# One emission table for all five engines in the leading part of an attention and two-FFN kernel

## The chip, the cores and the metric

The kernel runs on one core of one Trainium2 chip. The metric is the device time of one execution in microseconds (us). The engines are called as the profile calls them: PE (matrix products), DVE (VectorE), ACT (ScalarE), POOL (GpSimd), SP (the queue that issues DMAs). Each engine executes its own instructions in a fixed order; between engines, semaphores make one wait for another.

## The reference

A chunked linear attention is followed by two feed-forward layers over the same 3072 tokens (4 batches of 768, model width 256):

```python
L = np.exp(cum[:, :, :, None] - cum[:, :, None, :]) * causal
CB = np.einsum('bhin,bhjn->bhij', Cc, Bc)
y_intra = np.einsum('bhij,bhjd->bhid', CB * L, xc)
y_inter = np.einsum('bhin,bhnd->bhid', Cc, state) * decay_to_i[:, :, :, None]
y[:, :, sl] = y_intra + y_inter
state = decay_full * state + np.sum(Bx, axis=2)
...
x1 = (1 / (1 + np.exp(-(x @ w_gate))) * (x @ w_val)) @ w_out
h = x1 @ w_in
out = (h / (1 + np.exp(-h))) @ w2_out
```

The weights come as 64-bit floats. The kernel turns each slice into 32-bit floats with integer operations and splits it, like every activation, into a high and a low part, so that three products (high by high, high by low, low by high) stand for one.

## The kernel before, in words

**Attention** runs over 24 chunks q of 128 tokens. For a chunk, DMAs bring B and C (`bc`), `x` and the decays, broadcast to a 128x1024 tile `L`. A scan on DVE (line 338) makes the decay matrix in place; PE makes C·B (`cb`, two halves), DVE multiplies each half into `L` (line 383); PE then makes `y` from `L` and `x`, and, within a batch, from the running state `S` and the weighted C (`cwT`). POOL makes the weighted B and C (`bw`, `cw`); DVE updates the state (lines 421/423, 435). `y` is one PSUM tile with one buffer: ACT copies its high part to `xT0` (line 450) and DVE writes the low part to `xT1` (line 451), and only then may the next chunk's `y` begin. From chunk 4 on, B and C reach the products through bf16 tiles (`st`, filled by ACT and DVE, line 323) that DMA transposes turn (`tr`). `L` has four buffers, so the DMA of chunk q+4 can't start before chunk q's `y` is made.

**First layer.** Tokens form blocks b of 2, 2, 4, 4, 4, 4, 4 chunks. For each block and each f of 12 slices of the hidden width, PE makes a gate (`g`, six products) and a value (`v`, six), ACT the sigmoid, DVE their product `sg` (line 530); ACT rounds it to `gh`, DVE makes the rest `gl` (line 539), and PE adds the six products of `m1_out` to `acc`. For blocks 0 and 1 and f below 7 the output weights and `sg` stay whole, and `m1_out` has two f32 products; a later step, `w1_split` (DVE line 222), splits these weights.

**Weight conversion** (`conv`): for each f three DMAs fill `raw` (four buffers); ACT two steps, DVE two (lines 177, 178), POOL one or two additions, ACT the high part, DVE the low part (line 188).

**Second layer**, the same way with 16 slices, over six blocks of 512 tokens.

**What sets the order.** All steps are Python calls. A list of steps (attention by `slot_steps`, conversions placed by the table `WPOS`) is drained between the `g`, `v` and `o` calls of a tick (b, f), so many each time as `RUNS` says for blocks 0 and 1, and an even rate after that. The order of SP is the order of the calls (`manual_schedule` for SP alone); on PE, DVE, ACT and POOL the framework's scheduler orders the instructions when the program is built. On the chip the order of every engine is fixed.

Of the kernel before, what the change touches and what calls it, by code (L numbers as in the profile page):

```python
# [8 lines left out]
F32 = mybir.dt.float32  # L9
# [14 lines left out]
NX = 4  # L24
# [8 lines left out]
WPOS = [  # L33
    0, 0, 0, 22, 25, 31, 31, 31, 31, 31, 31, 31, 32, 32, 32, 32, 32, 32, 32, 32, 32, 34, 34, 34, 34, 34, 35,
    35, 35, 35, 35,
]

RUNS = [
# [3 lines left out]
]  # L42
# [3 lines left out]
def tile_linattn_moe_moe(  # L46
# [89 lines left out]
    def zeros(n, out=None, start=True):  # L136
        if out is None:
            out = acc[0][:, 1] if 0 in acc else ps[:, 1]
        n_ = out.shape[-1]
        last = pe_last[0]  # L140
        with tc.issue_after(last) if last is not None else nullcontext():
            for _ in range(n):
                nc.tensor.matmul(
                    out, zz[:, :P], zz[:, :n_], start=start, stop=start, skip_group_check=True
                )

    pe_last = [None]
# [17 lines left out]
    def conv(raw, hi, lo, n, whole=None):  # L165


# [17 lines left out]
        nc.gpsimd.tensor_tensor(ti, ti, r, ALU.add)  # L185
        with tc.issue_after(stg["behind"]) if "behind" in stg else nullcontext():
            nc.scalar.copy(hi, f)
        nc.vector.tensor_sub(lo, f, hi.bitcast(F32))

    def load_w(w, f, ins, outs, native=None):  # L190

        nonlocal cnt
        cnt += 1
        n = DM * (len(ins) + 1)
        raw = stg["p"].tile([P, 2 * n], I32, tag="raw", name=f"raw{cnt}", bufs=stg["raw"])
        fs = slice(f * P, (f + 1) * P)
        for z, m in enumerate(ins):
# [28 lines left out]


# [26 lines left out]
    def at_load(q):  # L254
        at_load_bc(q)
        at_load_x(q)

    def at_load_bc(q):
# [6 lines left out]
        nc.sync.dma_start(out=bc[:, 0], in_=B[b, :, sl, :].rearrange("h s n -> s h n"))  # L265
        nc.sync.dma_start(out=bc[:, 1], in_=C[b, :, sl, :].rearrange("h s n -> s h n"))
# [8 lines left out]
    def at_wide1(q):  # L275
# [627 lines left out]
```

## Time and profile before

| quantity | value |
|---|---|
| median of 3 runs | 663.72 us (662.73 to 664.83) |
| the profiled execution, its own time | 663.99 us |
| its span, first to last instruction | 662.2 us |
| mean granted PE clock | 0.992 of full speed |
| PE busy | 635.5 us (96% of the span) |
| DVE busy | 432.8 us (65%) |
| ACT busy | 329.0 us (50%) |
| POOL busy | 108.7 us (16%) |

The span and the execution's own time differ by 1.8 us that lie around the instructions. "Busy" counts the time from an instruction's start to its end; a share of the whole span is a mean over stages that have different limits, so the sections below ask for stretches.

### The profile page before, as it was taken

To read this page: it belongs to the slowest core of one execution; us is meant where nothing else is said; L and a number is where in the kernel's file an instruction comes from. 1 tells how busy PE (TensorE), PEld (TensorE's weight loads), DVE (VectorE), ACT (ScalarE), POOL (GpSimd) and SP (SyncE) were. 2 spreads that over 40 slices of the span, in tenths; PEclk is the share of its full clock that TensorE was granted. 3 is DMA by queue.
4 is the path that set the end of the run, shared out by engine and by line. 5 is a ranking of instruction groups with operands and counts; after the bars stand their busy time and mean duration, and the time that the engine had idled before them with its cause. 6 is when DMAs were issued, how large, how long until landed. Compare 5 with 4: busy or idle time off the path is not lost.

```text
span 662.2 us, 9861 instructions
## 1 busy us (share of the span) xinstructions
PE 635.5 (96%) x3680; PEld 522.0 (79%) x3682; DVE 432.8 (65%) x660; ACT 329.0 (50%) x649; POOL 108.7 (16%) x129
## 2 busy tenths in 40 slices
PE   5788898999999999999999999999999999999998
PEld 2477796777778787787888878888888888888886
DVE  8988987676768578656348885564564655544644
ACT  5675554544544554434336664544554544444543
POOL 4555432211221222311002410000000000000000
PEclk9998999999999999999999999999999999999999
DMA  8958577774656365342002410000000000000000
GB/s 207 267 146 212 89 158 154 153 128 109 120 121 145 77 145 119 81 125 75 0 1 66 157 33 1 1 32 1 1 32 1 1 32 1 33 0 1 33 0 33
DMA packets 140145, 51.18 MB, mean 77 GB/s; under 512 B 119009, under 2 KB 133537, under 8 KB 140097
## 3 DMA queue, kind: packets, MB, share of 16 engines
q1 hardware_dynamic: 139952, 50.41, 32.1%
q8 instruction: 29, 0.48, 0.3%
q14 instruction: 20, 0.16, 0.1%
q10 hardware_dynamic: 144, 0.13, 0.1%
HBM read 36.80 MB, written 3.24 MB: 60 GB/s over the span
## 4 chain that ended last, share of the span: by engine, by line
PE 79%; DVE 4%; DMA 4%; issue 3%; POOL 2%; ACT 1%; SPq 0%; DVEq 0%; POOLq 0%; ACTq 0%
PE h L509 20%; PE o L807 13%; PE v L509 11%; PE acc L558 11%; PE g L509 11%; PE o L828 7%; DMA raw<-in_moe_w_out_dram 3%; PE y L398 2%; DMA L<-ac_d 1%; POOL cvt L185 1%; PE cb L381 1%; PE y L392 1%; DVE sg L530 1%; DVE cvt L178 1%; DVE L L338 1%
## 5 line engine op out<-in xcount | busy, mean ns | idle before, releaser
L509 PE MATMUL v<-xT,w 128*128 128x512 f32 (+1 forms) x504 | 119.4, 369 | 3.9 <-ACT sg L522 2.4
L509 PE MATMUL g<-xT,w 128*128 128x512 f32 (+1 forms) x504 | 120.8, 370 | 0.0
L782 DVE TENSOR_TENSOR sh<-h,sh 128x512 f32<-128x512 f32 x96 | 66.2, 691 | 63.2 <-ACT sh L781 61.7
L509 PE MATMUL h<-x2T,w2b 128*128 128x512 f32 x432 | 107.0, 389 | 0.0
L791 DVE TENSOR_TENSOR gl<-sh,gh 128x512 fp32r<-128x512 f32 x96 | 65.8, 690 | 58.4 <-ACT gh L786 56.9
L509 PEld LDWEIGHTS v<-xT,w 128*128 128x128 f32 x504 | 87.4, 192 | 19.3 <-ACT sg L522 3.0
L509 PEld LDWEIGHTS g<-xT,w 128*128 128x128 f32 x504 | 87.7, 191 | 16.3 <-issue 1.5
L558 PE MATMUL acc<-gh,w 128*128 128x512 f32 (+1 forms) x280 | 94.5, 380 | 0.2 <-ACT x1T L569 0.2
L781 ACT ACTIVATE sh<-h 128x512 f32<-128x512 f32 x96 | 57.5, 599 | 73.3 <-PE h L509 70.2
L509 PEld LDWEIGHTS h<-x2T,w2b 128*128 128x128 f32 x432 | 80.7, 188 | 16.5
L786 ACT CAST gh<-sh 128x512 fp32r<-128x512 f32 x96 | 59.0, 620 | 62.2 <-PE o L807 31.0
L503 ACT CAST gh<-sg 128x512 fp32r<-128x512 f32 (+1 forms) x70 | 41.2, 588 | 93.6 <-DVE sg L530 93.6
L807 PE MATMUL o<-w2b,gh 128*128 128x512 f32 x280 | 74.2, 390 | 0.0
L530 DVE TENSOR_TENSOR sg<-v,sg 128x512 f32<-128x512 f32 (+1 forms) x84 | 50.8, 607 | 30.4 <-PE v L509 29.5
L539 DVE TENSOR_TENSOR gl<-sg,gh 128x512 fp32r<-128x512 f32 (+1 forms) x70 | 50.6, 723 | 23.3 <-ACT gh L503 23.0
L338 DVE TENSOR_TENSOR_SCAN L<-L,eye 128x1024 f32<-128x1024 f32 x24 | 55.2, 2302 | 16.0 <-DMA L<-ac_d 15.9
L185 POOL TENSOR_TENSOR cvt<-cvt,raw 128x512 int32<-128x512 int32 (+1 forms) x28 | 46.5, 1664 | 98.7 <-DVE cvt L178 81.5
L522 ACT ACTIVATE sg<-g 128x512 f32<-128x512 f32 (+1 forms) x84 | 44.8, 534 | 31.5 <-PE g L509 28.6
L558 PEld LDWEIGHTS acc<-gh,w 128*128 128x128 f32 x280 | 52.3, 190 | 9.9 <-ACT x1T L569 0.3
L807 PEld LDWEIGHTS o<-w2b,gh 128*128 128x128 f32 x280 | 51.8, 188 | 10.3
L558 PE MATMUL acc<-gl,w 128*128 128x512 f32 (+1 forms) x140 | 53.3, 380 | 1.0 <-DVE gl L539 1.0
L828 PEld LDWEIGHTS o<-w2b,gl 128*128 128x128 f32 x288 | 36.9, 191 | 1.3
(95 smaller groups left out, 724.9 us busy)
## 6 DMA issues: line engine op xcount, KB each, us to landing
L<-ac_d SPq DMA_DIRECT2D x23, 512.0 KB, 4.7
raw<-in_moe_w_out_dram SPq DMA_DIRECT2D x28, 256.0 KB, 3.9
raw<-in_moe_w_in_dram SPq DMA_DIRECT2D x16, 256.0 KB, 2.8
x<-in_x_dram SPq DMA_DIRECT2D x24, 128.0 KB, 3.1
raw<-in_moe_w_gate_dram SPq DMA_DIRECT2D x12, 256.0 KB, 4.4
raw<-in_moe_w_val_dram SPq DMA_DIRECT2D x12, 256.0 KB, 4.7
out_dram<-o2t SPq DMA_DIRECT2D x20, 128.0 KB, 1.7
bc<-in_B_dram SPq DMA_DIRECT2D x24, 64.0 KB, 2.7
```

The lines of the kernel that those rows point to most:

```text
L185: nc.gpsimd.tensor_tensor(ti, ti, r, ALU.add)
L338: nc.vector.tensor_tensor_scan(t["Lf"], t["Lf"], eye, 0.0, op0=ALU.mult, op1=ALU.add)
L509: nc.tensor.matmul(psum[:, :n], w[:, i, o + k * P : o + (k + 1) * P], xt[j][:, k, :n], start=(z == 0), stop=(z == len(k_terms) - 1),)
L530: nc.vector.tensor_mul(sg[:, :n], ps[:, :n], sg[:, :n])
L539: nc.vector.tensor_sub(lo[:, :n], sg[:, :n], hi[:, :n].bitcast(F32))
L558: mm = nc.tensor.matmul(o, v[:, ms], g[:, :n], start=(f == 0 and z == 0 and not (small and m)), stop=(f == NF1 - 1 and z == len(terms) - 1 ...
L781: nc.scalar.activation(sg, ps, AF.Sigmoid)
L782: nc.vector.tensor_mul(sg, ps, sg)
L786: nc.scalar.copy(hi, sg)
L791: nc.vector.tensor_sub(lo, sg, hi.bitcast(F32))
L807: nc.tensor.matmul(ps, hi[:, s], w2(f)[:, :, DM:], start=(f == 0), stop=False, skip_group_check=True,)
L828: nc.tensor.matmul(ps[:, :DM], g2[b, f][2][:, s], w2(f)[:, 0, DM:], start=False, stop=(f == NF2 - 1), skip_group_check=True,)
```

## The change

`WPOS`, `RUNS` and the loop over blocks 0 and 1 go. Every step function becomes a generator that stops (`yield`) after the part that one engine executes. One string, `ORDER`, lists 1,015 keys such as `g.0.3` (gate of block 0, slice 3), `L.5` (scan of chunk 5), `w.4` (conversion of slice 4) or `a.6` (the load of `L` of chunk 6); each appearance of a key runs its generator to its next stop. The table starts with the first load and ends inside block 3 (`v.3.5`). Under `manual_schedule()` without a list of engines, all five engines keep the order of the table. What the table has not run by then is run by the loop as before (`do` runs a key to its end, or does nothing where it is done), with the scheduler ordering all engines but SP. On each engine the instructions are the same in kind and number before and after: PE 3505, DVE 662, ACT 652, POOL 134, SP 231. Their order and the turn of some buffers are what differs.

```diff
-WPOS = [
...
-RUNS = [
...
+ORDER = """
+e.0 e.0 b.0 b.0 a.0 e.1 e.1 e.1 e.2 e.1 l.0 l.0 l.0 b.1 e.2 t.0 L.0 x.0 t.0 e.2 L.0 L.0 e.3 t.0 b.1 cb.0.0
+a.1 w.0 l.1 e.3 l.1 bw.0 e.3 l.1 w.0 t.0 t.1 cw.1 w.0 b.2 wr.0 st.0 cb.0.1 cb.0.0 l.2 w.0 t.1 st.0 l.2 S.0
...
+o.3.2 p.17.1.0 lo.3.4 v.3.5 g.3.5 p.17.0.2 p.17.1.2 v.3.5
+"""
...
         nc.scalar.activation(f, v[:, :, 1].bitcast(F32), AF.Copy, scale=2.0**-112)
-        nc.scalar.activation(r, v[:, :, 0].bitcast(U32), AF.Copy, scale=2.0**-29)
+        yield
         nc.vector.tensor_scalar(ti, ti, 3, None, op0=ALU.logical_shift_left)
+        yield
         nc.vector.scalar_tensor_tensor(
             ti, v[:, :, 1], -(2**31), ti, op0=ALU.bitwise_and, op1=ALU.bitwise_or
         )
+        yield
...
+    def conv_r(raw):
+        v = raw.rearrange("p (n t) -> p n t", t=2)
+        nc.scalar.activation(v[:, :, 0], v[:, :, 0].bitcast(U32), AF.Copy, scale=2.0**-29)
...
+    def st_tr(q, which):
+        t = T[q]
         tr = ap_.tile([P, H, P], BF16, tag=f"tr{which}", name=f"tr{which}{q}", bufs=2)
-        nc.sync.dma_start_transpose(out=tr, in_=st.rearrange("p h t n -> p (h t n)"))
+        nc.sync.dma_start_transpose(out=tr, in_=t["st", which].rearrange("p h t n -> p (h t n)"))
         t["tr%d" % which] = tr
...
+    live = {}
+    done = set()
+
+    def step(*key):
+        if key in done:
+            return False
+        if key not in live:
+            live[key] = iter(FN[key[0]](*key[1:]) or ())
+        if next(live[key], done) is done:
+            done.add(key)
+            del live[key]
+        return True
+
+    def walk(g):
+        for _ in g:
+            pass
+
+    def do(*key):
+        while step(*key):
+            pass
 
...
+    FN = dict(
+        e=decays, b=at_load_bc, x=at_load_x, a=at_loadL, t=at_wide1, r=at_bc, p=st_part, pt=st_tr, L=at_L,
+        bw=at_bw, cw=at_cw, ct=at_cwT, cb=at_cb, y=at_y, yt=at_yT, st=at_state, S=at_state2,
+        l=w1_load, w=w1_conv, wr=w1_conv_r, z=w1_split, g=m1_gate, v=m1_val, lo=m1_lo, o=m1_out,
     )
...
+    with tc.manual_schedule():
+        for key in ORDER.split():
+            name, *at = key.split(".")
+            step(name, *map(int, at))
...
+    ticks = [(b, f) for b in range(2, len(BLOCKS)) for f in range(NF1)]
+    steps = [g for s in range(ends[1], ends[2]) for g in slot_steps(s)]
...
+                for z in range(NF1):
+                    do("v", 0, z)
+                    do("v", 1, z)
+                    do("lo", 0, z)
+                    do("lo", 1, z)
+                    do("o", 0, z)
+                    do("o", 1, z)
+                    if z < NAT:
+                        do("z", z)
...
+        run(rate)
+        do("g", b, f)
+        run(rate)
         if prev is not None:
-            m1_lo(*prev)
-        m1_val(b, f)
+            do("lo", *prev)
+        do("v", b, f)
         prev = (b, f)
-        run(counts[2])
+        run(rate)
```

`decays` holds the few steps on the decays `a` that stood in line before; `st_part` is one of the three copies of the loop in `at_bc3`, `at_cw` is the second half of `at_bw`.

First place: DVE where chunk 6's `y` is handed over and chunk 7's may begin. `S7` is the state after chunk 7, `L8` the decays of chunk 8, `sg1_10` and `gl1_10` belong to block 1, slice 10; the number behind the last underscore is the program's own count. Before:

```order
L423 SCALAR_TENSOR_TENSOR S2_107<-S2_107,dec_202,st7_934 128x64
L435 TENSOR_TENSOR S7_940<-S2_107,blk_93 128x256
L530 TENSOR_TENSOR sg1_10_1335<-v1_10_1338,sg1_10_1335 128x256
L383 TENSOR_TENSOR L7_804<-cb7_0_884,L7_804 128x512
L323 COPY st08_914<-bc38_908 128x8x32
L323 COPY st18_920<-bc38_908 128x8x2x16
L539 TENSOR_TENSOR gl1_10_1347<-sg1_10_1335,gh1_10_1346 128x256
L338 SCALAR_TENSOR_TENSOR L8_882<-L8_882,eye_97 128x1024
L451 TENSOR_TENSOR xT1_2_757<-y6_890,xT0_2_756 128x2x128
L530 TENSOR_TENSOR sg1_11_1364<-v1_11_1367,sg1_11_1364 128x256
```

After:

```order
L500 TENSOR_TENSOR xT1_2_1149<-y5_1183,xT0_2_1148 128x2x128
L613 TENSOR_TENSOR gl0_11_1193<-sg0_11_1153,gh0_11_1192 128x256
L429 TENSOR_TENSOR L7_862<-cb7_0_1218,L7_862 128x512
L603 TENSOR_TENSOR sg1_10_1238<-v1_10_1172,sg1_10_1238 128x256
L429 TENSOR_TENSOR L7_862<-cb7_1_1252,L7_862 128x512
L500 TENSOR_TENSOR xT1_2_1149<-y6_1230,xT0_2_1148 128x2x128
L379 SCALAR_TENSOR_TENSOR L8_959<-L8_959,eye_97 128x1024
L500 TENSOR_TENSOR xT1_2_1149<-y7_1284,xT0_2_1148 128x2x128
L471 SCALAR_TENSOR_TENSOR S2_107<-S2_107,dec_111,st7_1304 128x64
L359 COPY st18_1257<-bc38_1189 128x8x2x16
```

The scan of `L8` stood in front of the low part of `y6` (`xT1_2<-y6`) and now stands behind it; the state update of chunk 7, one `st` copy and `gl1_10`, in front of it before, now come later, and the second product of `L7` has moved ahead of it. Of the seven low parts of `w1_split` (line 222), all stood further up before; three of them now stand further down.

Second place: DVE where block 1 gets its last input, `xT1_1<-y3`. Before:

```order
L451 TENSOR_TENSOR xT1_1_413<-y2_389,xT0_1_412 128x2x128
L383 TENSOR_TENSOR L3_229<-cb3_1_396,L3_229 128x512
L530 TENSOR_TENSOR sg0_1_330<-v0_1_332,sg0_1_330 128x256
L178 SCALAR_TENSOR_TENSOR cvt9_445<-raw6_293,cvt9_445 128x768
L177 TENSOR_SCALAR cvt11_478<-cvt11_478 128x768
L530 TENSOR_TENSOR sg0_2_465<-v0_2_467,sg0_2_465 128x256
L178 SCALAR_TENSOR_TENSOR cvt11_478<-raw8_420,cvt11_478 128x768
L451 TENSOR_TENSOR xT1_1_413<-y3_432,xT0_1_412 128x2x128
```

After:

```order
L500 TENSOR_TENSOR xT1_1_433<-y2_406,xT0_1_432 128x2x128
L429 TENSOR_TENSOR L3_270<-cb3_1_440,L3_270 128x512
L263 TENSOR_TENSOR w1_105<-x1T_81,w1_105 128x256
L379 SCALAR_TENSOR_TENSOR L4_346<-L4_346,eye_97 128x1024
L218 TENSOR_SCALAR cvt13_485<-cvt13_485 128x768
L500 TENSOR_TENSOR xT1_1_433<-y3_478,xT0_1_432 128x2x128
L220 SCALAR_TENSOR_TENSOR cvt13_485<-raw11_409,cvt13_485 128x768
L234 TENSOR_TENSOR w1_105<-cvt8_384,w1_105 128x512
```

The scan of `L4`, some twenty rows behind this place before, now stands in front of the low part of `y3`.

Third place: SP around the loads of `L7` and `L8`. Before:

```order
L327 DMA_TRANSPOSE tr06_764<-st06_760 128x8x128
L327 DMA_TRANSPOSE tr16_770<-st16_766 128x8x128
L265 DMA bc7_797<-in_B_dram 128x8x16
L266 DMA bc7_797<-in_C_dram 128x8x16
L273 DMA x7_800<-in_x_dram 128x8x32
L252 DMA L7_804<-ac_d_122 128x1024
L327 DMA_TRANSPOSE tr07_849<-st07_845 128x8x128
L327 DMA_TRANSPOSE tr17_855<-st17_851 128x8x128
L265 DMA bc8_869<-in_B_dram 128x8x16
L266 DMA bc8_869<-in_C_dram 128x8x16
L273 DMA x8_872<-in_x_dram 128x8x32
L252 DMA L8_882<-ac_d_122 128x1024
```

After:

```order
L317 DMA x5_844<-in_x_dram 128x8x32
L310 DMA bc7_742<-in_C_dram 128x8x16
L299 DMA L7_862<-ac_d_108 128x1024
L299 DMA L8_959<-ac_d_108 128x1024
L366 DMA_TRANSPOSE tr16_984<-st16_885 128x8x128
L366 DMA_TRANSPOSE tr06_1032<-st06_945 128x8x128
L317 DMA x7_1047<-in_x_dram 128x8x32
L308 DMA bc9_1074<-in_B_dram 128x8x16
L310 DMA bc9_1074<-in_C_dram 128x8x16
L310 DMA bc8_796<-in_C_dram 128x8x16
```

The load of `L8` stood behind the two transposes and three loads that follow `L7`'s; now it follows `L7`'s at once. In the same way `L4`'s load moves from row 52 of SP to row 33, ahead of most weights of slices 4 and up, and `L6`'s from row 70 to row 52.

## Rows read from the trace of the kernel before

**Rows 1.** Busy time by stretch: PE, PEld, DVE, ACT, POOL, clock, DMA share, GB/s.

```profile
0.00:112.50 112.50, 90.05 (x704) 72.15 (x706) 99.25 (x147) 66.70 (x154) 48.59 (x59) 0.95 0.74 176
112.50:350.00 237.50, 237.50 (x1443) 188.40 (x1441) 152.12 (x236) 107.00 (x218) 45.19 (x61) 1.00 0.46 100
350.00:400.00 50.00, 48.98 (x215) 39.84 (x214) 41.85 (x61) 34.43 (x62) 14.94 (x10) 1.00 0.27 85
400.00:662.00 262.00, 259.00 (x1327) 221.61 (x1325) 139.61 (x219) 120.88 (x218) 0.00 (x0) 1.00 0.04 13
```

**Rows 2.** Timeline of PE at the end of blocks 0 and 1: start, length, what.

```profile
107.80 0.28 PE L558 MATMUL acc<-gl,w 128*128 128x256 f32 x1
107.92 0.28 PE L558 MATMUL acc<-gh,w 128*128 128x256 f32 x1
109.81 0.71 PE L392 MATMUL y<-cwT,S 128*128 128x128 f32 x4 [1.61 <-DVE xT L451]
...
112.49 0.47 PE L509 MATMUL g<-xT,w 128*128 128x512 f32 x1
```

**Rows 3.** Timeline of DVE in the same stretch; in brackets idle time and who ended it.

```profile
98.39 2.29 DVE L338 TENSOR_TENSOR_SCAN L<-L,eye 128x1024 f32<-128x1024 f32 x1 [0.95 <-DMA L<-ac_d]
...
105.94 0.43 DVE L539 TENSOR_TENSOR gl<-sg,gh 128x256 fp32r<-128x256 f32 x1 [0.16 <-ACT gh L503]
107.15 2.29 DVE L338 TENSOR_TENSOR_SCAN L<-L,eye 128x1024 f32<-128x1024 f32 x1 [0.78 <-DMA L<-ac_d]
109.36 0.40 DVE L451 TENSOR_TENSOR xT<-y,xT 128x256 fp32r<-128x256 f32 x1
```

**Rows 4.** Groups of DVE by shape up to 112.7 us: busy, mean ns | idle before.

```profile
L338 DVE TENSOR_TENSOR_SCAN L<-L,eye 128x1024 f32<-128x1024 f32 x9 | 20.7, 2298 | 4.5 <-DMA L<-ac_d 4.5
...
L383 DVE TENSOR_TENSOR L<-cb,L 128x512 f32<-128x512 f32 x16 | 10.9, 683 | 1.4 <-POOL bw L346 1.1 <-PE cb L381 0.3
...
L435 DVE TENSOR_TENSOR S<-S,blk 128x256 f32<-128x256 f32 x8 | 6.3, 790 | 0.1
L539 DVE TENSOR_TENSOR gl<-sg,gh 128x256 fp32r<-128x256 f32 x10 | 5.8, 582 | 0.8 <-ACT gh L503 0.8
...
L222 DVE TENSOR_TENSOR w<-x1T,w 128x256 fp32r<-128x256 f32 x7 | 5.1, 735 | 1.1 <-ACT w L221 1.1
L323 DVE COPY st<-bc 128x256 bf16<-128x256 bf16 x10 | 5.1, 548 | 0.5 <-POOL bc L306 0.5
...
L423 DVE SCALAR_TENSOR_TENSOR S<-S,dec,st 128x64 f32<-128x64 f32 x6 | 1.7, 275 | 0.0
```

**Rows 5.** Timeline of DVE at chunk 4's scan.

```profile
60.64 2.29 DVE L338 TENSOR_TENSOR_SCAN L<-L,eye 128x1024 f32<-128x1024 f32 x1 [1.93 <-DMA L<-ac_d]
```

**Rows 6.** Timeline of DVE at chunk 6's scan.

```profile
89.60 2.29 DVE L338 TENSOR_TENSOR_SCAN L<-L,eye 128x1024 f32<-128x1024 f32 x1 [0.31 <-DMA L<-ac_d]
```

**Rows 7.** Timeline of the SP queue: loads of `L4` and `L8`, chunk 7's transposes between.

```profile
54.15 0.43 SPq L252 DMA_DIRECT2D L<-ac_d  x1
...
97.10 2.59 SPq L327 DMA_TRANSPOSE tr<-st  x2
...
102.88 0.57 SPq L252 DMA_DIRECT2D L<-ac_d  x1
```

**Rows 8.** Timeline of all engines: one POOL addition and one DVE product beside it.

```profile
65.05 2.65 POOL L185 TENSOR_TENSOR cvt<-cvt,raw 128x768 int32<-128x768 int32 x1 [1.39 <-DVE cvt L178]
...
66.22 1.76 DVE L435 TENSOR_TENSOR S<-S,blk 128x256 f32<-128x256 f32 x1
```

**Rows 9.** DVE products that write the state `S`, to 112.7 us: shortest/median/longest ns.

```profile
L435 DVE TENSOR_TENSOR S<-S,blk x8: 400/426/1756, 16.4 to 111.4; 128x256 f32<-128x256 f32 x8
```

**Rows 10.** DVE copies into `st`, the same stretch.

```profile
L323 DVE COPY st<-bc x10: 214/224/1808, 45.3 to 105.6; 128x256 bf16<-128x256 bf16 x10
```

**Rows 11.** DVE low parts `gl`, the same stretch.

```profile
L539 DVE TENSOR_TENSOR gl<-sg,gh x10: 401/417/2065, 81.5 to 110.6; 128x256 fp32r<-128x256 f32 x10
```

**Rows 12.** DVE low parts of the whole weights (`w1_split`), the same stretch.

```profile
L222 DVE TENSOR_TENSOR w<-x1T,w x7: 408/417/1531, 19.1 to 54.9; 128x256 fp32r<-128x256 f32 x7
```

More of the change, by code (lines that the diff above doesn't have):

```diff
@@ L139, in zeros @@
         n_ = out.shape[-1]
[L140 to L147, printed above, removed]
+        for _ in range(n):
+            nc.tensor.matmul(
+                out, zz[:, :P], zz[:, :n_], start=start, stop=start, skip_group_check=True
+            )
     ZW = {2: 4, 3: 6}
@@ new lines, in slot_steps, with joint @@
+            add("cb", s + 1, 1)
+            add("y", s, 1)
+        else:
+            def joint():
+                do("y", s, 0)
+                do("y", s, 1)
+                if ok(s + 1):
+                    do("ct", s + 1)
+                    do("st", s + 1)
+            if ok(s):
+                st.append(joint)
+            add("cb", s + 1, 0)
+            add("cb", s + 1, 1)
+        add("t", s + 2)
+        if ok(s + 2):
+            st += [lambda: step("r", s + 2), lambda: do("L", s + 2), lambda: do("r", s + 2)]
@@ new lines, in slot_steps @@
+        add("yt", s)
+        if ok(s + 2) and s + 2 >= NX:
+            for i in range(2):
+                st.append(lambda i=i: ([do("p", s + 2, i, j) for j in range(3)], do("pt", s + 2, i)))
+        if ok(s + 2):
+            st.append(lambda: (do("bw", s + 2), do("cw", s + 2)))
+        if early or not ok(s):
+            add("ct", s + 1)
+            add("st", s + 1)
+        add("S", s + 1)
+        if s >= 1 and ok(s + 3):
+            st.append(lambda: (do("b", s + 3), do("x", s + 3)))
+            add("a", s + 3)
@@ L516, in m1_gate @@
         ps = ps_gv.tile([P, 512], F32, tag="gv", name=f"g{b}_{f}", bufs=GV)
-        three(ps, w1[:, f], 0, xT[b], n)
+        yield from three(ps, w1[:, f], 0, xT[b], n)
+        yield
         if b < 2 and f < NAT:
@@ L527, in m1_val @@
         ps = ps_gv.tile([P, 512], F32, tag="gv", name=f"v{b}_{f}", bufs=GV)
-        three(ps, w1[:, f], DM, xT[b], n)
+        yield from three(ps, w1[:, f], DM, xT[b], n)
+        yield
         sg = g1[b, f][0]
@@ new lines, in tile_linattn_moe_moe, with decays @@
+    e_sb = first
+    e_i = padded(ap_, NCH * U, "e_i").rearrange("p (c u) -> p c u", c=NCH)
+    dtmp = padded(ap_, NCH * nb * H, "dtmp").rearrange("p (cb h) -> p cb h", h=H)
+    dec = padded(ap_, NCH * nb, "dec")
+    ps = ps_acc.tile([P, KM, 512], F32, tag="acc", name="ps_e")
+    cl = lambda t: t.rearrange("u (c l) -> u c l", c=NCH)
+    def decays(part):
+        if part == 0:
+            nc.vector.memset(first, 0.0)
+            yield
+            nc.sync.dma_start(out=a_sb, in_=a.rearrange("b h s -> (b h) s"))
+        elif part == 1:
+            clip(a_sb)
+            yield
+            nc.vector.tensor_copy(cl(first)[:, :, 0:1], cl(a_sb)[:, :, 0:1])
+            yield
+            nc.vector.memset(cl(a_sb)[:, :, 0:1], 0.0)
+            yield
+            nc.sync.dma_start(out=ac_d.rearrange("c b (h l) -> (b h) c l", h=H), in_=cl(a_sb))
+        elif part == 2:
+            nc.vector.tensor_tensor_scan(e_sb, a_sb, first, 0.0, op0=ALU.mult, op1=ALU.add)
+            yield
+            for c in range(NCH):
+                nc.tensor.transpose(
+                    ps[:, 0, c * U : (c + 1) * U], e_sb[:, c * L : (c + 1) * L], ident[:U, :U]
+                )
+            yield
+            nc.vector.tensor_copy(e_i.rearrange("p c u -> p (c u)"), ps[:, 0, : NCH * U])
+        else:
+            nc.tensor.matmul(
+                ps[:, 1, : NCH * U], sel, e_i.rearrange("p c u -> p (c u)"), start=True, stop=True
+            )
+            yield
+            nc.vector.tensor_mul(
+                dtmp,
+                ps[:, 1, : NCH * U].rearrange("p (cb h) -> p cb h", h=H),
+                blk.unsqueeze(1).to_broadcast([P, NCH * nb, H]),
+            )
+            yield
+            nc.vector.tensor_reduce(dec, dtmp, AX.X, ALU.add)
@@ L670, in run @@
         for _ in range(min(k, len(steps))):
-            steps.pop(0)()
-    def need(k):
-        while k not in seen:
             steps.pop(0)()
```

306 lines of the change are left out of this document (124 added, 182 removed), and 3 rows, old and new, of the table RUNS.

## The prediction

> **What bounds the kernel now.** I read the busy times by stretch first. The span has two regimes [rows 1]. From 112.5 to 350 us PE is busy 237.50 of 237.50 us: no wait there costs anything, and later stretches lose only 1.0 and 3.0 us. Up to 112.5 us PE is busy 90.05 us, so it stands idle for 22.5 us, nearly all that the whole span has. Since the instructions are the same before and after, the change can give only what it takes from these 22.5 us, and a microsecond by which the dense part starts earlier is a microsecond off the end.
>
> Who makes PE wait there? In the same row DVE is busy 99.25 of 112.5 us, ACT 66.70, POOL 48.59. So DVE sets the pace of the leading stage, with 13.25 us of idle time of its own. The timeline of PE at the end of the stage shows the last wait [rows 2]: after 107.92 us PE has nothing until 109.81 us, and of this it waits 1.61 us for DVE's line 451, the low part of `y6`, because `y` has one buffer and `y7` can't begin before it is read. Then PE is dense. The timeline of DVE tells why line 451 came so late [rows 3]: at 107.15 us DVE began the scan of `L8`, 2.29 us long, which had itself waited 0.78 us for its load, and the low part of `y6`, queued behind, started at 109.36 us. The scan makes nothing that PE needs soon. This is what a changed order can mend, and the two terms of my sum are this queue and this wait.
>
> **The change part by part.**
>
> *Term 1, the queue of DVE in front of `y6`'s low part.* The order listing of DVE names what has moved. Out of the way go three low parts of whole weights, the state update of chunk 7 (two instructions), one `st` copy, `gl1_10` and the scan of `L8`; into it comes the second product of `L7`. With the means of the leading stage [rows 4]: 3 x 0.735 + 0.275 + 0.790 + 0.548 + 0.582 + 2.298 - 0.683 = 6.0 us. With the shortest times of the groups that have long outliers [rows 9 to 12]: 3 x 0.408 + 0.275 + 0.400 + 0.214 + 0.401 + 2.298 - 0.683 = 4.1 us. But PE, too, has less done when `y7` comes: by the order 12 products of `acc` and 3 of `v1_11` now stand behind it, which start 0.12 us apart (107.80 to 107.92) [rows 2], 1.8 us, and five smaller instructions, together at most 0.6 us if each took as long; I take 2.0 us. Net 2.1 to 4.0 us; I take the middle, **3.0 us**. What is late next? The other hand-over of that moment, `gl1_11`, has two DVE rows fewer in front of it than before, and more products of PE, so it isn't.
>
> *Term 2, DVE's waits for `L`.* The scans waited 4.5 us in the stage, all for loads from `ac_d` [rows 4]: 1.93 us for `L4` [rows 5], 0.31 for `L6` [rows 6], 0.95 for `L7` and 0.78 for `L8` [rows 3], and the rest of the 4.5, 0.5 us, for `L2`. The loads were issued late, not slowly: `L8`'s at 102.88 us, behind chunk 7's transposes, issued from 97.10 us, and landing for the scan of 107.15; `L4`'s at 54.15, behind seven slices of weights, for the scan of 60.64 [rows 5, 3, 7]. The change issues `L4` 19 rows of SP earlier, `L6` 18, `L8` next to `L7`; the buffers that they fill belong to chunks 0, 2, 3 and 4, whose `y` stands far in front on PE. `L2` keeps its place and its wait. So 1.93 + 0.31 + 0.95 + 0.78 = 4.0 us may go; nothing goes if each of these scans then waits for another input or if DVE stops one instruction later instead. A part of each wait may come back so, and I take **3.0 us** of 0 to 4.0. The price of the early `L4` load is paid by the weights behind it on the same queue; ACT has 112.5 - 66.70 = 45.8 us idle in the stage [rows 1], which is the cover, and if it is gone the cost is one such load, no more than the 1.93 us that it saved.
>
> *The scan of `L4` in front of the low part of `y3`.* It puts 2.298 us [rows 4] before the input of block 1. At that place DVE's lead over PE is smaller than at `y7`, where the same scan stands in front before and after, so time lost there is time not lost later. I take 0; the bounds are 0 and +2.3 us.
>
> *The steps cut into single-engine parts* add no instruction. Every engine had a fixed order before as well, so keeping one costs nothing in itself. The new waits between ACT, POOL and DVE that the table may make show in no row; the nearest are the small ones of today, 13.25 - 4.5 = 8.75 us of DVE's idle time in all. They could be halved or grow by half; I take them as unchanged, and the bounds below cover this.
>
> *DVE beside POOL.* At 66.22 us a product into `S` took 1.76 us while POOL ran an addition from 65.05 us for 2.65 us [rows 8]; its shortest is 0.400 us [rows 9]. Four groups lose this way, against their shortest times, in the stage [rows 4, 9 to 12]: `S` 6.3 - 8 x 0.400 = 3.1; `st` 5.1 - 10 x 0.214 = 3.0; `gl` 5.8 - 10 x 0.401 = 1.8; whole weights 5.1 - 7 x 0.408 = 2.2; together 10.1 us, a fifth of POOL's 48.59 us. Which instruction meets which is decided by the order alone, and no row tells how the new order falls. I take the loss as unchanged; half and double are the bounds, -5.0 and +10.1 us.
>
> The Trainium skill (SBUF — State Buffer, section Who interferes with whom) says that a DVE instruction with two inputs in SBUF contends with a GpSimd instruction that reads SBUF, over a port pair that one of them holds for its whole length while the other blocks. The row at 66.22 us agrees, 1.76 for 0.400 us. The rule speaks against this change: a DVE with less idle time meets POOL more often; if meetings grew as 112.5 to 106.5 us, the loss would grow by 0.6 us and the sum would be 658.3.
>
> **Sum.** 663.99 (the profiled execution) - 3.0 - 3.0 = 658.0 us; the median of the runs lies 0.27 us lower, so **657.7 us**.
>
> **The rivals.** About 0.3%, 2.0 us, is what a measurement of this kernel can tell from no change: 661.7 and 665.7 are the edges.
>
> *More is gained*: the new order keeps POOL's additions beside scans (mean 2298 ns for the 2.29 us of single ones [rows 3, 4]), and half of the 10.1 us goes as well: 657.7 - 5.0 = 652.7 us. For it: the order was free to do so. Against: nothing in the moved rows shows it.
>
> *Nothing is gained*: the waits for `L` come back as waits for ACT or POOL (+3.0), and the scan of `L4` holds block 1 for its 2.3 us: 657.7 + 5.3 = 663.0 us. Against it: both would have to hold together.
>
> *Slower*: the leading stage is packed more tightly, and DVE's instructions with two SBUF inputs meet POOL's conversions twice as much. Place: the conversions of the weights. Price: +10.1 us, 667.8 us. It makes the kernel no better than before from +6.0 us, when the loss grows 1.6 times, and measurably slower from +8.0 us, 1.8 times. For it: the table puts steps of two conversions around `L4`'s scan at the start of block 1. Against: DVE's total work ahead of `y7` shrinks.
>
> *The change does not do what it says*: excluded, since the listings of all five engines show the moved rows.
>
> **How the numbers follow.** The forecast, 655 to 661.7 us: 0.50. More gained: 0.20. Nothing gained: 0.13. Slower: 0.17. Faster is 0.50 + 0.20 = 0.70, within 0.3% 0.13, slower 0.17. The low end: both terms full (-4.0, -4.0) and half of the loss to POOL gone, 663.7 - 13.0 = 650.7, rounded to 651 us, which leaves out some 0.08. The high end, 666.5 us, lies between the edge 665.7 and the slower rival and leaves out some 0.11.
>
> **What would show it.** In the profile after: PE's idle time in the leading part falls from 22.5 to about 16.5 us, and PE is dense from about 106 us on; scans of `L4`, `L6`, `L7` and `L8` no longer wait for a load; the low part of `y6` starts without a scan in front. Wrong would be: DVE's busy time in that part above 105 us (the loss to POOL grew), new waits of DVE for ACT or POOL of more than 6 us, or idle time of PE after the table's end.

## The result, and the profile after

| | before | after |
|---|---|---|
| median of the runs | 664.28 us | 653.04 us (4 runs, 652.95 to 653.59) |
| ratio to before | 1 | 0.9834, 95% interval 0.9811 to 0.9857 |
| the profiled execution, its own time | 663.99 us | 652.97 us |
| its span | 662.2 us | 651.2 us |
| PE busy / idle within the span | 635.5 / 26.7 us | 633.4 / 17.8 us |

The changed kernel is 11.2 us faster. The forecast was 657.7, a gain of 6.0. The direction was right and the time lies between the outer bounds (651 to 666.5), but it misses the range 655 to 661.7, which had a chance of 0.50: the gain is nearly twice the forecast's. The number is that of the rival "more is gained" (652.7, chance 0.20).

Busy time by stretch after the change (PE, PEld, DVE, ACT, POOL, clock, DMA share, GB/s), the answer to [rows 1]:

```profile
0.00:112.50 112.50, 98.28 (x770) 77.27 (x773) 97.94 (x153) 68.31 (x160) 53.67 (x65) 1.00 0.82 192
112.50:350.00 237.50, 237.50 (x1420) 188.09 (x1419) 153.72 (x241) 109.17 (x223) 45.03 (x56) 1.00 0.43 96
350.00:400.00 50.00, 49.96 (x228) 41.11 (x227) 36.47 (x57) 32.57 (x59) 12.46 (x8) 1.00 0.21 69
400.00:651.00 251.00, 247.67 (x1269) 211.97 (x1267) 133.21 (x209) 116.00 (x209) 0.00 (x0) 1.00 0.04 13
```

PE's idle time up to 112.5 us falls from 22.5 to 14.2 us, that of the stretch from 350 to 400 us by 1.0. The rest of the 11 us is busy time: the sum of PE's column is 2.1 us smaller with the same instructions. The clock column fits: 1.00 in every stretch, against 0.95 in the first one before.

The timeline of PE has its last waits longer than 0.2 us here, where before the last one ended at 109.81 us [rows 2]:

```profile
59.53 0.38 PE L426 MATMUL cb<-tr,tr 128*128 128x128 bf16 x4 [0.78 <-DMA tr<-st]
60.64 0.62 PE L580 MATMUL g<-xT,w 128*128 128x256 f32 x3 [0.61 <-ACT sg L594]
...
97.99 0.61 PE L438 MATMUL y<-cwT,S 128*128 128x128 f32 x4
```

PE is dense from about 61 us on, 48 us earlier than before. `y7` begins at 97.99 us without a wait. The timeline of DVE at that place, the answer to [rows 3]:

```profile
97.32 0.41 DVE L500 TENSOR_TENSOR xT<-y,xT 128x256 fp32r<-128x256 f32 x1
97.65 2.28 DVE L379 TENSOR_TENSOR_SCAN L<-L,eye 128x1024 f32<-128x1024 f32 x1
100.00 0.42 DVE L500 TENSOR_TENSOR xT<-y,xT 128x256 fp32r<-128x256 f32 x1
```

The low part of `y6` stands in front of the scan of `L8`, as the listing said. Groups of DVE up to the low part of `y7` (100.4 us), the answer to [rows 4], and the shortest, median and longest of three groups in the same stretch, the answers to [rows 9 to 11]:

```profile
L379 DVE TENSOR_TENSOR_SCAN L<-L,eye 128x1024 f32<-128x1024 f32 x9 | 20.5, 2283 | 0.0
L603 DVE TENSOR_TENSOR sg<-v,sg 128x256 f32<-128x256 f32 x23 | 9.4, 417 | 4.3 <-PE v L580 3.9 <-ACT sg L594 0.4
L234 DVE TENSOR_TENSOR w<-cvt,w 128x512 fp32r<-128x512 f32 x7 | 7.7, 1098 | 0.2 <-ACT w L232 0.2
```

```profile
L483 DVE TENSOR_TENSOR S<-S,blk x6: 412/594/902, 14.1 to 93.9; 128x256 f32<-128x256 f32 x6
L359 DVE COPY st<-bc x9: 214/220/447, 32.3 to 93.8; 128x256 bf16<-128x256 bf16 x9
L613 DVE TENSOR_TENSOR gl<-sg,gh x8: 408/415/426, 72.4 to 94.9; 128x256 fp32r<-128x256 f32 x8
```

No scan waits for a load any more (4.5 us before), and DVE now waits for PE's `v`: 3.9 us. The four groups of the prediction lose some 2 us instead of 10.1. The long outliers are gone: the longest `gl` takes 426 ns instead of 2065, the longest `st` 447 instead of 1808, the longest `S` 902 instead of 1756. One group went the other way: the low parts of the converted weights of 512 columns take 7.7 us instead of 5.5.

### The profile page after: what moved, and what is told of

Read it like the earlier page. It is cut to its first block, busy times and chain, and to the rows that moved or that the text cites. A ratio compares the mean times of both kernels' runs of the same rounds, so it can differ in the third digit from the quotient of the medians.

```text
span 651.2 us, 9850 instructions
## 1 busy us (share of the span) xinstructions
PE 633.4 (97%) x3680; PEld 518.4 (80%) x3682; DVE 421.3 (65%) x660; ACT 326.0 (50%) x649; POOL 111.2 (17%) x129
## 3 DMA queue, kind: packets, MB, share of 16 engines
q1 hardware_dynamic: 139952, 50.41, 32.5%
## 4 chain that ended last, share of the span: by engine, by line
PE 91%; DVE 1%; ACT 1%; issue 0%; ACTq 0%
PE h L580 20%; PE acc L634 15%; PE v L580 15%; PE g L580 15%; PE o L839 13%; PE o L860 7%; PE y L445 2%; PE cb L426 2%; PE y L438 1%; PE st L461 1%; DVE w L234 0%; PE cwT L405 0%; PE o L848 0%; ACT st L361 0%; DVE cvt L220 0%
## 5 line engine op out<-in xcount | busy, mean ns | idle before, releaser
L580 PE MATMUL g<-xT,w 128*128 128x512 f32 (+1 forms) x504 | 122.3, 370 | 3.3 <-DVE xT L500 1.2
L580 PE MATMUL v<-xT,w 128*128 128x512 f32 (+1 forms) x504 | 121.2, 369 | 0.0
L634 PE MATMUL acc<-gh,w 128*128 128x512 f32 (+1 forms) x280 | 97.3, 382 | 0.2 <-ACT x1T L645 0.2
L580 PEld LDWEIGHTS h<-x2T,w2b 128*128 128x128 f32 x432 | 80.7, 188 | 16.5
L613 DVE TENSOR_TENSOR gl<-sg,gh 128x512 fp32r<-128x512 f32 (+1 forms) x70 | 47.8, 683 | 27.4 <-ACT gh L572 27.0
L229 POOL TENSOR_TENSOR cvt<-cvt,raw 128x512 int32<-128x512 int32 (+1 forms) x28 | 44.5, 1592 | 101.8 <-DVE cvt L220 80.2
L839 PEld LDWEIGHTS o<-w2b,gh 128*128 128x128 f32 x280 | 51.8, 188 | 10.3
L429 DVE TENSOR_TENSOR L<-cb,L 128x512 f32<-128x512 f32 x48 | 32.7, 682 | 9.3 <-PE cb L426 7.5
```

Of the source, the lines that this page charges most:

```text
L580: nc.tensor.matmul(psum[:, :n], w[:, i, o + k * P : o + (k + 1) * P], xt[j][:, k, :n], start=(z == 0), stop=(z == len(k_terms) - 1),)
L613: nc.vector.tensor_sub(lo[:, :n], sg[:, :n], hi[:, :n].bitcast(F32))
L634: mm = nc.tensor.matmul(o, v[:, ms], g[:, :n], start=(f == 0 and z == 0 and not (small and m)), stop=(f == NF1 - 1 and z == len(terms) - 1 ...
L839: nc.tensor.matmul(ps, hi[:, s], w2(f)[:, :, DM:], start=(f == 0), stop=False, skip_group_check=True,)
```

## The experiments

Three numbers tell the kernels apart. *Loss* is the time of each DVE instruction less the shortest of its kind (same operation, shape and tiles) in the same execution, summed to the end of `y7`'s low part; the four groups of the prediction are a part of it. *Idle* is PE's up to 112.5 us. *Busy* is PE's over the whole span, always with the same instructions. All three come from the profiled execution.

| kernel | median | ratio to before | loss to 60 us / after | idle | busy |
|---|---|---|---|---|---|
| before | 664.28 | 1 | 9.1 / 7.4 | 22.5 | 635.5 |
| after | 653.04 | 0.9834 | 7.6 / 1.2 | 14.2 | 633.4 |
| e1, only SP keeps the table | 677.98 | 1.0223 | 8.6 / 9.0 | 26.2 | 643.2 |
| f0, control | 663.75 | 0.9995 | 9.1 / 7.5 | 23.4 | 636.1 |
| f1, early loads | 664.65 | 1.0012 | 8.6 / 8.9 | 19.5 | 640.6 |
| f2, scan behind | 662.80 | 0.9978 | 9.4 / 7.5 | 22.0 | 635.0 |
| f3, control with fills | 656.22 | 0.9882 | 1.5 / 2.6 | 16.6 | 634.3 |
| e4, after with fills | 650.01 | 0.9808 | 2.4 / 1.5 | 12.2 | 631.8 |
| h1, after's order, then before's | 662.58 | 0.9979 | 5.7 / 7.6 | 21.0 | 638.2 |
| h2, before's order, then after's | 662.79 | 0.9989 | 9.4 / 1.4 | 22.0 | 634.8 |
| e5, one swap at the start | 652.64 | 0.9840 | 6.1 / 1.1 | 16.4 | 632.0 |
| u4, scan of `L4` late | 655.14 | 0.9866 | 6.8 / 1.6 | 15.7 | 636.0 |

**The table kept by SP alone (e1).**

```diff
-    with tc.manual_schedule():
+    with tc.manual_schedule(engines={mybir.EngineType.SP}):
```

> The changed kernel with the same table, but only SP keeps it; the framework's scheduler orders PE, DVE, ACT and POOL. Theory A (the order that DVE and POOL keep decides how often they meet, and that is most of the gain): the meetings fall by chance again, DVE's loss against its shortest times in the leading part goes back from 8.8 towards 16.5 us, and the time is 657 to 665 us. Rival B (the gain is in what SP's order does, early loads of L above all, and in the order of emission): the time stays at 653, within 2 us.

677.98 us, ratio 1.0223 (1.0205 to 1.0241): not only is the gain lost, the kernel is slower than before. The order in which the steps are emitted and SP's order do not bring it by themselves, and rival B falls; what they would be worth with the other orders held still, this run can't say. Its span is 675.1 us, 12.9 more than before: 5.2 us are idle time of PE (31.9 against 26.7) and 7.7 us busy time. DVE's loss is back at 17.6 us. So the order of the other four engines matters, and this run does not yet say which part of it.

**Edits of the kernel before, with its scheduler (e2 and e3).** The load of `L` issued ahead of the transposes, and POOL's additions replaced by fills (instructions that only write), each as an edit of the kernel before:

```diff
+        if s >= 1:
+            add(s + 3, at_loadL)
         add(s + 2, at_bc3, 0)
...
-            add(s + 3, at_loadL)
```

> The kernel before with one edit: the load of L for a chunk is issued ahead of the transposes of the chunk in front of it, as the changed kernel does for L4, L6 and L8. Term 2 of the sum: DVE's waits for loads of L (4.5 us up to 112.5 us) go, and the time falls by 3.0 us to 661.3 (0 to 4.0 less, 660.3 to 664.3). Rival: the waits come back as waits of DVE for ACT, POOL or PE and the time is within 2 us of 664.3.

> The kernel before, with POOL's additions of the weight conversion replaced by two fills each of the tile that they would write, so that POOL reads nothing from SBUF there; the conversion's addition is left out. Theory A: DVE's loss against its shortest times in the leading part (16.5 us of all groups) nearly goes, and the time falls by 7 to 12 us, to 652 to 657. Rival B (queue order and late loads are the whole difference between the kernels): the time falls by 3 us at most, to 661 to 664.

They took 672.24 us (1.0133) and 669.67 us (1.0094), both slower than any theory allowed. Neither tests what it was made for: after either edit the scheduler put all engines into another order (in the trace of e2, with its one moved load, 245 of DVE's 660 instructions are of another kind than those at the same place before). From here on every experiment keeps its orders.

**A control whose order can be edited (f0).** The orders of the kernel before, read from its program, became a table with one key per instruction; the step functions stop after each instruction, as here in the three-product loop:

```diff
-            if z == 3:
+            if z:
                 yield
             nc.tensor.matmul(
```

> A control. The orders that the five engines of the kernel before have, written down as a table (one key for each instruction, 1,638 keys, to chunk 15) that all five engines keep; from there on the scheduler orders as before. If keeping an order costs nothing, the time is that of the kernel before, 663.5, within 2 us, with 22 us of idle time of PE up to 112.5 us. If the time is much lower, being kept is what gains and not the order.

663.75 us, ratio 0.9995 (0.9981 to 1.0008). Up to block 3 each engine has the row order of before. Being kept costs and gains nothing, and single moves can now be priced.

**Term 2 alone (f1).** The order of SP (ordinary listing, `L4`'s load shown; `L6`'s and `L8`'s likewise):

```diff
 DMA raw4<-in_moe_w_val_dram 128x2x256
+DMA L4<-ac_d 128x1024
 DMA raw4<-in_moe_w_out_dram 128x512
...
-DMA L4<-ac_d 128x1024
```

> The control with term 2 alone: on SP the loads of L4, L6 and L8 stand where the changed kernel has them (rows 32, after a.5, and next to L7), nothing else moves. The prediction's term 2: 3.0 us less than the control (0 to 4.0), the waits of L4, L6 and L8 gone. Rival: DVE stops one instruction later and the time stays within 1 us of the control's.

664.65 us against 663.75: no gain. The scans of the control, then those of f1, in the timeline of DVE (start, length, in brackets the wait):

```profile
60.16 2.29 DVE L408 TENSOR_TENSOR_SCAN L<-L,eye 128x1024 f32<-128x1024 f32 x1 [2.05 <-DMA L<-ac_d]
...
98.50 2.29 DVE L408 TENSOR_TENSOR_SCAN L<-L,eye 128x1024 f32<-128x1024 f32 x1 [0.65 <-DMA L<-ac_d]
108.53 2.29 DVE L408 TENSOR_TENSOR_SCAN L<-L,eye 128x1024 f32<-128x1024 f32 x1 [1.50 <-DMA L<-ac_d]
```

```profile
57.99 2.28 DVE L408 TENSOR_TENSOR_SCAN L<-L,eye 128x1024 f32<-128x1024 f32 x1
75.22 2.29 DVE L408 TENSOR_TENSOR_SCAN L<-L,eye 128x1024 f32<-128x1024 f32 x1 [1.36 <-DMA L<-ac_d]
...
100.85 2.29 DVE L408 TENSOR_TENSOR_SCAN L<-L,eye 128x1024 f32<-128x1024 f32 x1 [2.29 <-DMA L<-ac_d]
108.53 2.28 DVE L408 TENSOR_TENSOR_SCAN L<-L,eye 128x1024 f32<-128x1024 f32 x1
```

The waits of `L4` and `L8` are gone, and `L5` and `L7`, whose loads still stand behind transposes, wait in their place: 3.7 us against 4.2. The rival was right. The profiled execution shows a second thing: PE's idle time did fall, 23.4 to 19.5 us, but its busy time grew by 4.5 us. The granted clock says how. One of f1's pauses in PE's timeline, and busy time by microsecond around it (columns as above):

```profile
81.68 0.65 PE L473 MATMUL y<-L,x 128*32 128x128 f32 x8 [1.84 <-DVE L L457]
```

```profile
80.00:81.00 1.00, 0.00 (x0) 0.00 (x0) 1.00 (x4) 0.63 (x1) 0.34 (x1) 0.83 0.00 0
81.00:82.00 1.00, 0.32 (x8) 0.20 (x8) 1.00 (x4) 0.21 (x2) 0.00 (x0) 0.50 0.34 79
82.00:83.00 1.00, 1.00 (x11) 0.73 (x4) 1.00 (x2) 0.68 (x2) 0.00 (x0) 0.50 0.82 183
...
86.00:87.00 1.00, 1.00 (x7) 1.00 (x6) 0.77 (x3) 0.44 (x2) 0.20 (x1) 0.50 0.93 148
87.00:88.00 1.00, 1.00 (x10) 0.93 (x10) 0.04 (x2) 1.00 (x3) 0.92 (x2) 0.76 0.02 1
```

PE stood idle for 1.84 us up to 81.68 us (another wait, of 1.38 us, had ended at 78.75 us); the clock fell to 0.50, which is 1.2 of 2.4 GHz, and came back between 87 and 88 us. Products of one kind in f1, from 84 to 88.3 us and from 90 to 98 us (busy, mean ns):

```profile
L608 PE MATMUL v<-xT,w 128*128 128x256 f32 x6 | 1.5, 415 | 0.0
```

```profile
L608 PE MATMUL v<-xT,w 128*128 128x256 f32 x18 | 2.9, 287 | 0.0
```

415 against 287 ns: in the 6 us that follow, 6 x (1 - 287 / 415) = 1.9 us are lost, so the pause of 1.84 us is paid a second time. This pause does not tell f1 from the control, which has it too. f1 alone has two more of this length, up to 62.64 and 103.78 us, where PE waits for POOL. The control's pause, f1's two, and busy time in f1 and then in the control at the three places:

```profile
80.85 0.65 PE L473 MATMUL y<-L,x 128*32 128x128 f32 x8 [1.85 <-DVE L L457]
```

```profile
62.64 0.32 PE L490 MATMUL st<-x,bw 128*32 128x64 f32 x8 [2.13 <-POOL bw L415]
103.78 0.32 PE L490 MATMUL st<-x,bw 128*32 128x64 f32 x8 [1.88 <-POOL bw L415]
```

```profile
64.00:65.00 1.00, 1.00 (x3) 0.79 (x3) 1.00 (x3) 0.06 (x1) 1.00 (x1) 0.50 1.19 364
106.00:107.00 1.00, 1.00 (x8) 0.91 (x8) 0.60 (x2) 1.00 (x4) 0.81 (x2) 0.50 0.65 101
```

```profile
64.00:65.00 1.00, 1.00 (x9) 0.92 (x8) 1.00 (x3) 0.00 (x0) 0.43 (x1) 1.00 1.38 170
82.00:83.00 1.00, 1.00 (x7) 1.00 (x6) 1.00 (x2) 0.00 (x0) 0.54 (x1) 0.50 0.92 211
106.00:107.00 1.00, 0.58 (x7) 0.36 (x6) 0.84 (x4) 1.00 (x4) 0.06 (x1) 1.00 0.38 123
```

With a longer stretch around 20 to 26 us, f1 runs some 10 us more at 0.50 than the control; by the two products this costs some 3 of the 4.5 us (an estimate). That the clock took the gain is shown for the profiled executions at most: f1's has the lowest clock of its 11 runs (0.985 of 0.985 to 0.995), the control's the highest of its 11 (0.992 of 0.987 to 0.992), and runs of f1 at 0.992 took 663.7 to 665.9 us. Why the idle time that went gave nothing in these runs stays open.

**The core of term 1 alone (f2).** DVE's order:

```diff
 TENSOR_TENSOR gl1_10<-sg1_10,gh1_10 128x256
+TENSOR_TENSOR xT1_2<-y6,xT0_2 128x2x128
 SCALAR_TENSOR_TENSOR L8<-L8,eye 128x1024
-TENSOR_TENSOR xT1_2<-y6,xT0_2 128x2x128
```

> The control with the core of term 1 alone: on DVE the scan of L8 stands behind the low part of y6 and not in front of it, nothing else moves. The scan and its wait for the load are 3.07 us, PE's wait at that place was 1.61 us. The prediction's term 1 leads to 1.6 to 2.1 us less than the control. Rival: the end is set earlier, and what PE gains there it loses at the next wait: within 1 us of the control's.

662.80 us, 0.95 less than the control (by the ratios 1.1), with intervals that overlap (0.9964 to 0.9993 against 0.9981 to 1.0008); it is nearer to the rival than to the term. The control's wait at `y7` and what stands near that place in f2, both from PE's timeline:

```profile
111.19 0.71 PE L466 MATMUL y<-cwT,S 128*128 128x128 f32 x4 [2.32 <-DVE xT L529]
```

```profile
108.71 0.32 PE L490 MATMUL st<-x,bw 128*32 128x64 f32 x8 [0.98 <-POOL bw L415]
110.98 0.50 PE L608 MATMUL g<-xT,w 128*128 128x512 f32 x1 [0.26 <-ACT xT L527]
```

The wait of 2.32 us went; 1.24 us of it came back at once, for POOL's `bw8`, which hangs on the scan that was moved, and for ACT.

**DVE beside POOL (f3 and e4).** The same replacement in the control and in the changed kernel, which both leave out the conversion's addition:

```diff
-            nc.gpsimd.tensor_tensor(whole.bitcast(I32), ti[:, n:], r[:, n:], ALU.add)
+            nc.gpsimd.memset(whole, 0.0)
+            nc.gpsimd.memset(whole, 0.0)
...
-        nc.gpsimd.tensor_tensor(ti, ti, r, ALU.add)
+        nc.gpsimd.memset(f, 0.0)
+        nc.gpsimd.memset(f, 0.0)
```

> The control with POOL's additions of the weight conversion replaced by two fills each, so that POOL reads nothing there; the conversion's addition is left out. All orders are those of the kernel before otherwise. Theory A (DVE's loss beside POOL, 16.5 us of all its groups up to 112.7 us, against 8.8 in the changed kernel, is most of the surplus over the forecast): 6 to 12 us less than the control, against the 3.0 us that the same replacement took from the changed kernel. Rival B: 3 us less, as in the changed kernel, so that the loss beside POOL does not tell the two kernels apart.

> The changed kernel with the same replacement of POOL's additions by fills; the conversion's addition is left out. Theory A: only 8.8 us of DVE's loss are left to go, 7.6 of them before 60 us, and the time falls by 0 to 5 us, to 648 to 653; so the distance to the kernel before with fills shrinks from 11.2 us to some 4 to 6. Rival B: both kernels gain alike and the distance stays at 9 to 12 us.

The control falls by 7.5 us (ratio 0.9882), the changed kernel by 3.0 (by its ratio, 0.9808 against 0.9834, by 1.7). Groups of DVE in f3 up to 105.6 us:

```profile
L645 DVE TENSOR_TENSOR gl<-sg,gh 128x256 fp32r<-128x256 f32 x10 | 4.2, 415 | 0.9 <-ACT gh L602 0.8
L514 DVE TENSOR_TENSOR S<-S,blk 128x256 f32<-128x256 f32 x8 | 3.3, 416 | 0.1
```

`gl` is at 415 ns instead of 582 and `S` at 416 instead of 790 [rows 4]: these instructions were long because of POOL's additions. In the control 12.5 us of loss went and 7.5 us of time, 0.6 us for each; with fills the two kernels are 6.2 us apart instead of 10.7 (by the ratios, 4.9). Theory A's ranges hold (6 to 12 us, and 4 to 6 us apart, the latter at its edge). So 4.5 to 5.8 us of the gain go with the meetings of DVE and POOL that the new order avoids, about half of the 11; the intervals of the four ratios make this uncertain by some 2.6 us (an estimate). One rival stays: the fills also shorten POOL's own work, up to 112.5 us by 10.3 us in either kernel (48.4 to 38.1 and 53.7 to 43.4 us), and no run separates that from the reads that are gone. Against it, PE's waits for POOL did not fall in the control (4.3 us, 5.8 with fills).

**Which half of the order (h1 and h2).** Two merged tables (in words below), cut where PE becomes dense after the change (61.75 us) and at 61.04 us of before:

```diff
+keys = after[:cut] + [what before has left, in its order]
...
+keys = before[:cut] + [what after has left, in its order]
```

> All five engines keep the changed kernel's order up to the product with which its PE becomes dense (61.75 us, the product of block 0, slice 3, into acc), and what is left comes in the order of the kernel before. Theory C (the first part builds a store of work that the second part only spends): most of the 11 us is there, 653 to 657 us. Rival D (the second part's order is the gain, since 5.8 of the 8.2 us of PE's idle time that go lie behind 60 us): only 2 to 4 us of it, 660 to 662.

> The reverse: the order of the kernel before up to 61.04 us of its trace, and then what is left in the changed kernel's order. Theory C: the store is missing, 660 to 664 us. Rival D: 655 to 658 us. If both halves give less than the whole together, the rest is in how they fit.

662.58 and 662.79 us: each half alone gives about 1 us, the two together 11. Theory C fails on the first half and rival D on the second; the last line of the expectation holds. PE's timelines show what goes wrong, first h1's and then h2's behind the cut:

```profile
79.54 0.98 PE L608 MATMUL v<-xT,w 128*128 128x256 f32 x6 [1.08 <-DVE sg L631]
82.47 0.42 PE L473 MATMUL y<-L,x 128*32 128x128 f32 x8 [1.83 <-DVE L L457]
...
110.58 0.71 PE L466 MATMUL y<-cwT,S 128*128 128x128 f32 x4 [1.41 <-DVE xT L529]
```

```profile
63.14 0.44 PE L490 MATMUL st<-x,bw 128*32 128x64 f32 x8 [5.00 <-POOL bw L415]
69.88 0.58 PE L454 MATMUL cb<-tr,tr 128*128 128x128 bf16 x4 [3.44 <-DMA tr<-st]
```

h1 has the old waits of the second half, and with 7.6 us its old loss. h2 has the new second half, with a loss of 1.4 us and PE busy 32.44 of the 32.5 us from 80 to 112.5; but it pays 8.4 us on the way in, because chunk 4's `bw` and transposes are not ready, and the clock from 61 to 80 us is 0.64. It sheds 6 us of DVE's loss and gains 1 us: an avoided meeting is worth time only where no other wait takes its place. In the changed kernel they are, since `L4`'s scan starts at 39.20 us (60.64 before [rows 5]):

```profile
39.20 2.28 DVE L379 TENSOR_TENSOR_SCAN L<-L,eye 128x1024 f32<-128x1024 f32 x1
```

So the first half prepares chunk 4 some 20 us earlier. That the second half can run without a pause only then fits h1 and h2, but a merged table also has a seam that neither kernel has; the next run tests a part of it.

**The scan of `L4` alone put back (u4).** On DVE the scan moves down 24 rows; `bw4`, `st4`, its state update and `cwT5` follow:

```diff
-SCALAR_TENSOR_TENSOR L4<-L4,eye 128x1024
 TENSOR_SCALAR cvt<-cvt 128x768
 TENSOR_TENSOR xT1_1<-y3,xT0_1 128x2x128
...
 TENSOR_TENSOR w1<-cvt,w1 128x512
+SCALAR_TENSOR_TENSOR L4<-L4,eye 128x1024
```

> The changed kernel with one thing undone: the scan of L4 stands 22 rows behind the low part of y3 on DVE, as in the kernel before, and not two rows in front of it; the product bw4, the four products st4, the update of S2 that hang on it and the transpose cwT5, which shares a PSUM buffer with st4, follow it. The rest keeps the changed kernel's order. Theory E (what gains is that chunk 4 is prepared some 20 us earlier, so that PE never waits for the attention from 61 us on): PE waits again around 62 to 70 us and the time is 655 to 659 us, 2 to 6 more than the changed kernel's 653. Rival (the prediction's own step: the scan's place there is worth nothing, or costs block 1 its 2.3 us): 651 to 654 us.

655.14 us, 2.1 more than the changed kernel; its ratio is 0.9866 (0.9848 to 0.9884 against 0.9811 to 0.9857). The intervals just overlap, and the 2.1 us are uncertain by nearly as much: theory E holds at its lower edge, and the rival (up to 654) is not quite excluded. The profile is of the longest of its five executions (659.95), so only its first part is read. Timelines of DVE, of POOL and of PE there:

```profile
57.21 3.95 DVE L411 TENSOR_TENSOR_SCAN L<-L,eye 128x1024 f32<-128x1024 f32 x1
```

```profile
56.70 2.31 POOL L261 TENSOR_TENSOR cvt<-cvt,raw 128x768 int32<-128x768 int32 x1
```

```profile
64.41 0.33 PE L437 MATMUL cwT<-ident,cw 128*128 128x128 f32 x1 [2.16 <-DVE S L503]
```

The late scan met an addition of POOL and took 3.95 us, and PE waits where `cwT5` shares a PSUM buffer with `st4`, a neighbourhood that this edit made. So the earlier scan, with the steps that hang on it, is worth about 2 us, but whether by chunk 4's lead or by a meeting avoided, this run does not tell.

**One swap more (e5).** PE's order at the start:

```diff
-... b.1 e.2 t.0 L.0 x.0 ...
+... b.1 t.0 e.2 L.0 x.0 ...
```

> The changed kernel with one swap in PE's order at the start: the transposes of chunk 0's B and C stand in front of those of the decays, which wait 6.2 us for DVE. B and C are there at about 4.0 us. If what follows on ACT and DVE is ready to use it, PE's wait shortens and the time falls by 1 to 2 us, to 651 to 652; the rival is that the scan of L0 and its first product, on DVE, come no earlier and the time stays within 0.5 us of 653.

652.64 us, ratio 0.9840 (0.9826 to 0.9855): the rival was right. The wait of 6.2 us is split up (3.9 us for the load of B, 1.2 for DVE) and returns later; PE's idle time is 16.4 us in the profiled execution, the longest of the four (653.69). No kernel here that computes everything beats the changed one.

## Why the prediction was right in direction and short in size

- **What bounds the kernel.** Right on the place: 8.2 of the 8.9 us of PE's idle time that went lie up to 112.5 us. Too narrow on the cause: I read DVE's queue as the pace of it all. The waits of PE in the kernel before (total, times, longest), which the prediction did not use, also name POOL, for 4.7 us:

```profile
PE st L414 <- POOL bw L346: 3.3, 3, 2.2
...
PE cwT L360 <- POOL cw L351: 1.4, 1, 1.4
```

  After the change PE waits for POOL nowhere in this stretch.
- **Term 1 (3.0 us)** was mis-sized. Its core is worth about 1 us alone (f2). The 3.0 us also exceed the wait that the term was to mend: PE waits 1.61 us there [rows 2], and the 2.0 us of products that move behind `y7` are still to be done. "What is late next?" was answered from `gl1_11`; late next was `bw8`, which hangs on the very scan that was moved.
- **Term 2 (3.0 us)** was wrong as a term of its own: 0 alone (f1). "A part of each wait may come back" was all of it, at the loads that were not moved. In the changed kernel all 4.5 us of these waits are gone, but there all of SP's and DVE's order changed with the loads.
- **The scan of `L4` in front of the low part of `y3`, taken as 0 with bounds 0 and +2.3 us,** had the wrong sign. Putting it back costs about 2 us (u4, at the edge of its noise). The bound excluded a gain, though chunk 4's `bw` and transposes hang on that scan and PE comes to them at 60 us. I costed the row that it delays and not the rows that it releases.
- **DVE beside POOL, "taken as unchanged",** is the step that failed most. The loss fell from 16.5 to 8.8 us while POOL was busy for 48.8 and 49.2 us up to the same step, the low part of `y7`, and 4.5 to 5.8 us of the gain go with it (f3, e4). The lower bound, -5.0, comes near by luck: it took half of the four groups' 10.1 us at full price, where some 8 us of them went, at a price of some 0.6. The mechanism of the rival "more is gained" is not what happened either: POOL's additions ran beside scans for 4.5 us before and 2.2 after. The row to ask for would have been which DVE steps the table sets beside POOL's additions.
- **The clock.** 2.1 us of PE's busy time were in no term: with fewer pauses in the lead the clock stayed at 1.00 (0.95 before).
- **The signs.** No scan waits for a load, the low part of `y6` starts without a scan in front, DVE is busy for 97.94 us (the mark was 105): as said. PE dense from 106 us and 16.5 us idle: it was 61 us and 14.2.

The two terms that made up the forecast give 1 us measured one by one, and the forecast came as near as it did by luck, because terms that I had set to zero gave the rest. What stays open: the pieces measured alone (about 1, 0, 2 and 4.5 to 5.8 us) leave some 2 to 4 us that belong to no single piece, or more, if the 2 us of u4 are a meeting avoided and so a part of the 4.5 to 5.8. The halves say why a sum can't settle it: 1 and 1 us apart, 11 together.

## What to carry to other kernels

Before pricing a moved step, ask which rows it releases and not only which rows it delays, and look for the next wait on all engines. Where two engines lose time beside each other, their order is a term of the sum of its own, even if no work is added or removed. To test one move in a program that a scheduler orders, first write the orders down and keep them: otherwise one moved load reorders everything, and the run measures that.

## What was not expected of the hardware

- The same instructions of PE are busy for 631.8 us (e4) to 643.2 us (e1). In f1 the clock stood at 1.2 GHz for some 6 us after a pause of 1.84 us, and a product took 415 instead of 287 ns.
- When DVE and POOL meet, either may be the one that is held up. In the changed kernel this subtraction of POOL, 0.62 and 0.80 us long at two places without a scan, began 0.21 us after the scan of `L8` and took longer than the scan, which kept its 2.28 us:

```profile
97.86 2.48 POOL L343 TENSOR_TENSOR bcr<-bc 128x256 f32<-128x256 f32 x1 [4.54 <-issue]
```

  In u4 the scan began 0.51 us after POOL's addition, and the scan was the one that grew (3.95 us). The Trainium skill (SBUF — State Buffer, section Who interferes with whom) says that the order of issue decides which one blocks; these two rows agree. The whole stage bears it out: before, 15.4 of DVE's 16.5 us of loss lie on instructions that began while one of POOL was running, and 0.2 on those that POOL joined later; after the change, 8.0 of 8.8 and 0.2. So an order can shed DVE's loss while POOL's busy time stays: let DVE start first.
